# The first ninth of w1 in eight transfers of every eighth partition, instead of one transfer of 128 partitions

## The chip, the cores and the metric

One core of one Trainium2 chip runs the kernel. The metric is the device time of one execution in microseconds (us). The kernel before takes 136.42 us (median of 6 runs, 136.31 to 136.55). A run has a state, fast or slow; a run that is over 1.5% above the fastest of its kernel counts as slow. A ratio here is the mean time of one kernel's fast runs over the mean time of the other's fast runs of the same rounds, so it is not quite the ratio of the medians that are quoted. The span of a profile (134.6 us before) leaves out some 1.8 us at the ends.

## The reference, cut to what matters

One token passes through an attention branch and a feed-forward branch, mixed by a gate. All inputs are bfloat16.

```
x: [1, 1, 576]
g = sigmoid(sum(x * gate_w))
q = x @ wq                         # wq [576, 4096]
a = softmax(q k / sqrt(128)) v @ wo  # 16 KV heads, the last 4096 keys of each; wo [4096, 576]
h = gelu(x @ w1 + b1)              # w1 [576, 4608], 5.3 MB
b = h @ w2 + b2                    # w2 [4608, 576]
return g * a + (1 - g) * b
```

In all 53.6 MB have to be read once: K and V 33.6 MB, the four weights 20 MB. There is nearly no reuse, and reading sets the time: the profile below shows the DMA engines full from 4 us on, at 411 to 431 GB/s in the stretches listed up to 12 us.

## The kernel before: the parts that matter here

Four tiny loads go out on the scalar queue, all large ones on the sync queue, in this order. The first 512 rows of w1 are laid out as partition p, part k (row 4p + k). Each part is one load of 128 partitions x 4608 elements, 9216 B in a row.

```python
nc.scalar.dma_start(out=x_row[:], ...)      # 1 x 576
nc.scalar.dma_start(out=gw_row[:], ...)     # 1 x 576
nc.scalar.dma_start(out=b2_row[:], ...)     # 1 x 576
nc.scalar.dma_start(out=b1_t[:], ...)       # 128 x 2 x 18, runs of 36 B
...
w1_m = w1_t[:, 0 : KM * F].rearrange("p (k n) -> p k n", k=KM)        # KM = 4, F = 4608
w1_src = B_w1[0:DM, :].rearrange("(p k) n -> p k n", k=KM)
for k in range(KM):
    nc.sync.dma_start(out=w1_m[:, k, :], in_=w1_src[:, k, :])          # 1.18 MB each
nc.sync.dma_start(out=w1_l, ...)            # the last 64 rows of w1, 0.59 MB
... # wq: two loads of 2.1 MB, one of 0.5 MB; then 8 K loads, 8 V loads of 2.1 MB, w2 and wo
for r in range(0, RO, 8):                   # wo, late in the kernel: 4 loads of 1.18 MB, rows of 9216 B
    nc.sync.dma_start(out=wo_t[:, r : r + 8, :], in_=wo_src[:, r : r + 8, :])
```

The product h = x @ w1 uses part k for 36 matmuls, and each of them needs all 128 partitions of the part. So splitting a part by partitions does not let any product start earlier.

The framework that schedules the kernel gives each transfer on the sync and scalar queues one of eight completion semaphores, in turn. A transfer whose semaphore is still held by an earlier one waits in its issuing queue until that one has landed: in the kernel before the first wq load waited 2.7 us for w1 part 0, and the first K load 5.1 us for b1; by the trace each of the two pairs is on one semaphore.

## Time and profile before

| what | before |
|---|---|
| time | 136.42 us |
| bytes read | 53.6 MB, 398 GB/s over the span |
| first w1 row starts to move | 1.74 us |
| w1 part 0 has landed | 5.95 us |
| last large landing on the chain, then the tail | 127.47 us, then about 5 us of row products |

The view by stretches of the kernel before comes first. Its columns are the stretch in us and its length, busy us (and instructions) of each engine, then the granted TensorE clock, the mean busy share of the 16 DMA engines and the GB/s they moved. A packet, the piece that one engine moves at a time, counts whole in the stretch in which it starts.

```profile
1.00:2.00 1.00, 0.00 (x0) 0.00 (x0) 0.03 (x1) 0.00 (x0) 0.97 (x4) 1.00 0.34 66
2.00:4.00 2.00, 0.47 (x5) 0.31 (x5) 0.66 (x3) 1.71 (x2) 1.39 (x5) 1.00 0.91 309
4.00:6.00 2.00, 0.00 (x1) 0.01 (x1) 0.17 (x1) 1.53 (x1) 0.00 (x0) 1.00 0.99 416
6.00:8.00 2.00, 2.00 (x32) 2.00 (x33) 2.00 (x12) 0.00 (x0) 0.00 (x0) 1.00 1.01 416
8.00:10.00 2.00, 1.58 (x19) 1.48 (x17) 0.11 (x2) 0.00 (x0) 0.00 (x0) 1.00 1.05 431
10.00:12.00 2.00, 2.00 (x28) 1.79 (x29) 0.98 (x4) 0.17 (x1) 0.00 (x0) 1.00 0.99 411
...
100.00:120.00 20.00, 10.09 (x219) 7.80 (x217) 0.48 (x2) 0.00 (x0) 0.00 (x0) 0.50 1.00 420
```

From 4 us on the last two columns hardly move: the DMA engines are full, at 411 to 431 GB/s in these stretches. TensorE is idle for half of the stretch from 100 to 120 us. The kernel is bound by its loads, and no gap comes later in which a late start could be made up.

The timeline of the sync queue shows how little issuing it took to get there. Columns: start, busy us, queue, line, transfer, count.

```profile
0.74 2.03 SPq L77 DMA_DIRECT2D w_t<-in_B_w_dram  x4
2.82 0.47 SPq L78 DMA_DIRECT2D w_t<-in_B_w_dram  x1
5.97 0.82 SPq L85 DMA_DIRECT2D wq_t<-in_A_wq_dram  x2
6.83 0.46 SPq L86 DMA_DIRECT2D wq_t<-in_A_wq_dram  x1
```

By 3.3 us all 5.3 MB of w1, 12.5 us of transfer at 425 GB/s, are in the queue. Two lines, from the view of line 77 and from the waits of the sync queue, matter later:

```profile
L77 SPq DMA_DIRECT2D w_t<-in_B_w_dram x4: 384/426/649, 0.7 to 2.1; - x4
...
SPq L276 <- DMA b_t<-in_B_b_dram: 5.1, 1, 5.1
```

The first gives the duration of an issue (least, median, most, in ns). The second says that the first K load waited 5.1 us for the landing of b1 (256 packets of 36 B), whose semaphore it takes over. This wait cost nothing, as some 5.8 MB were still queued ahead when it ended. The chain of waits ends like this (start, us, what):

```profile
100.23 27.19 DMA w_t<-in_B_w_dram
127.47 0.28 PE ya_ps L184
```

### The profile page before, as it was taken

Reading aid. Unit: us, or ns where it says so; the run is one execution under the profiler, and the core shown is the slowest. Engines: PE = TensorE matmul, PEld = TensorE weight load, DVE = VectorE, ACT = ScalarE, POOL = GpSimd, SP = SyncE. Lnnn points to the kernel's source line nnn. Section 1 sums busy time; section 2 is a strip of 40 time slices with the busy share of each in tenths; the row PEclk is TensorE's granted clock in tenths of the full one; section 3 lists DMA queues with packets and bytes.
Section 4 is the critical chain, followed back from the end, with each engine's and each line's share of the span. In section 5 each row is a group of like instructions: output and inputs, shape, how many; then the busy total and the mean of one; then the engine's idle time right before and its main releaser. Section 6 shows DMA issues by size and latency. Waiting matters only on the chain.

```text
span 134.6 us, 2438 instructions
## 1 busy us (share of the span) xinstructions
PE 92.4 (69%) x1116; PEld 57.9 (43%) x1116; DVE 50.3 (37%) x65; ACT 6.8 (5%) x11; POOL 2.8 (2%) x13
## 2 busy tenths in 40 slices
PE   1289989570499798979679219799752253798692
PEld 0285983470133233323233018765652253455461
DVE  2242013012958999998984845200000000100001
ACT  3600000001000000000000060000000000000001
POOL 8000000000000000000000000000000000000000
PEclk9999999999999999999999975557975555569999
DMA  4999999999999999999999999999999999999940
GB/s 121 417 424 428 421 443 414 427 420 429 429 429 424 424 433 419 433 414 443 414 443 407 438 425 446 400 438 409 438 414 429 424 411 424 416 416 427 401 170 0
DMA packets 5041, 53.76 MB, mean 400 GB/s; under 512 B 804, under 2 KB 808, under 8 KB 1448
## 3 DMA queue, kind: packets, MB, share of 16 engines
q1 hardware_dynamic: 4754, 53.61, 94.8%
q8 instruction: 8, 0.13, 0.4%
q10 hardware_dynamic: 278, 0.01, 0.1%
q14 instruction: 1, 0.01, 0.0%
HBM read 53.62 MB, written 0.00 MB: 398 GB/s over the span
## 4 chain that ended last, share of the span: by engine, by line
DMA 69%; PE 14%; DVE 6%; issue 5%; SPq 3%; ACTq 1%; ACT 0%; DVEq 0%
DMA w_t<-in_B_w_dram 36%; DMA kv_t<-in_A_k_cache_dram 26%; DMA b_t<-in_B_b_dram 8%; DVE early L297 6%; PE s_ps L303 5%; PE ya_ps L184 4%; PE yb_ps L185 4%; SPq L400 2%; PE o_ps L384 1%; SPq L276 1%; ACTq L63 0%; ACT out_row L422 0%; ACTq L67 0%; ACTq L65 0%; DVEq L297 0%
## 5 line engine op out<-in xcount | busy, mean ns | idle before, releaser
L303 PE MATMUL s_ps<-early 128*128 128x512 bf16 x128 | 32.9, 404 | 11.3 <-DVE early L297 11.3
L297 DVE STREAM_TRANSPOSE early<-kv_t 128x2048 f32<-128x2048 f32 x16 | 35.8, 2286 | 5.4 <-DMA kv_t<-in_A_k_cache_dram 3.4
L303 PEld LDWEIGHTS <-early 128*128 128x128 bf16 x128 | 12.9, 100 | 30.9 <-issue 17.4
L384 PE MATMUL o_ps<-pt,kv_t 128*128 128x4 bf16 x512 | 15.0, 166 | 14.5 <-DMA kv_t<-in_A_v_cache_dram 10.8
L384 PEld LDWEIGHTS <-kv_t 128*128 128x128 bf16 x512 | 14.7, 103 | 15.2 <-DMA kv_t<-in_A_v_cache_dram 11.1
L194 PE MATMUL h_ps<-xt,w_t 128*128 128x1 bf16 x144 | 9.6, 201 | 3.6 <-DMA w_t<-in_B_w_dram 3.6
L406 DVE TENSOR_TENSOR om<-o_ps,rh 128x128 bf16<-128x128 f32 x1 | 0.3, 292 | 30.1 <-PE o_ps L384 30.1
L184 PE MATMUL ya_ps<-w_t,gt 128*1 128x288 bf16 x36 | 10.6, 324 | 1.4 <-DMA w_t<-in_B_w_dram 1.4
L194 PEld LDWEIGHTS <-w_t 128*128 128x128 bf16 x144 | 9.3, 162 | 4.7 <-DMA w_t<-in_B_w_dram 3.7
L185 PE MATMUL yb_ps<-w_t,gt 128*1 128x288 bf16 x36 | 10.5, 322 | 0.0
L184 PE MATMUL ya_ps<-wo_t,ov 128*1 128x288 bf16 x32 | 9.6, 328 | 0.7 <-DMA wo_t<-in_A_wo_dram 0.7
L185 PE MATMUL yb_ps<-wo_t,ov 128*1 128x288 bf16 x32 | 9.5, 326 | 0.0
L421 DVE CAST out_row<-ya_ps 1x288 bf16<-1x288 f32 x1 | 0.4, 446 | 16.1 <-PE ya_ps L184 16.1
L235 PE MATMUL q_ps<-xt,wq_t 128*128 128x1 bf16 x128 | 3.7, 165 | 1.8 <-DMA wq_t<-in_A_wq_dram 1.8
L185 PEld LDWEIGHTS <-gt 128*1 128x1 bf16 x36 | 3.4, 94 | 3.5 <-issue 1.6
L235 PEld LDWEIGHTS <-wq_t 128*128 128x128 bf16 x128 | 3.6, 104 | 2.7 <-DMA wq_t<-in_A_wq_dram 1.9
L337 ACT ACTIVATE early<-s_ps,negm 128x1024 bf16<-128x1024 f32 x2 | 2.2, 1108 | 47.2 <-DVE negm L332 47.2
L184 PEld LDWEIGHTS <-gt 128*1 128x1 bf16 x36 | 3.4, 94 | 2.0
L185 PEld LDWEIGHTS <-ov 128*1 128x1 bf16 x32 | 3.0, 95 | 2.4 <-issue 0.6
L184 PEld LDWEIGHTS <-ov 128*1 128x1 bf16 x32 | 3.0, 95 | 2.2 <-DVE ov L414 0.4
L285 PE MATMUL s_ps<-no_r,no_l 1*128 1x512 bf16 x8 | 3.6, 620 | 0.4 <-DVE hx L213 0.4
L213 DVE TENSOR_TENSOR hx<-h_ps,b_t 128x36 f32<-128x36 f32 x1 | 0.2, 196 | 8.1 <-PE h_ps L203 8.1
(78 smaller groups left out, 36.2 us busy)
## 6 DMA issues: line engine op xcount, KB each, us to landing
kv_t<-in_A_k_cache_dram SPq DMA_DIRECT2D x8, 2048.0 KB, 25.1
kv_t<-in_A_v_cache_dram SPq DMA_DIRECT2D x8, 2048.0 KB, 14.9
w_t<-in_B_w_dram SPq DMA_DIRECT2D x4, 1152.0 KB, 10.1
wo_t<-in_A_wo_dram SPq DMA_DIRECT2D x4, 1152.0 KB, 21.8
wq_t<-in_A_wq_dram SPq DMA_DIRECT2D x2, 2048.0 KB, 16.1
w_t<-in_B_w_dram SPq DMA_DIRECT2D x1, 2592.0 KB, 20.7
w_t<-in_B_w_dram SPq DMA_DIRECT2D x1, 1296.0 KB, 27.2
w_t<-in_B_w_dram SPq DMA_DIRECT2D x2, 576.0 KB
```

The source lines that it names most:

```text
L184: nc.tensor.matmul(ya_ps[:], lhsT=vec, rhs=row[:, 0:NH], start=start, stop=stop, skip_group_check=True)
L185: nc.tensor.matmul(yb_ps[:], lhsT=vec, rhs=row[:, NH:D], start=start, stop=stop, skip_group_check=True)
L194: nc.tensor.matmul(h_ps[:, c : c + 1], lhsT=w1_m[:, k, f0 : (c // NJ + 1) * FB : NJ], rhs=xt[:, k : k + 1], start=(k == 0 and c == 0), sto ...
L235: nc.tensor.matmul(q_ps[:, j : j + 1], lhsT=wq_m[:, k, j * Dh : (j + 1) * Dh], rhs=xt[:, k : k + 1], start=(k == 0 and j == 0), stop=False ...
L276: nc.sync.dma_start(out=t[:], in_=cache[0, 2 * i : 2 * i + 2, Sk - W : Sk, :].rearrange("h (p c) d -> p h (c d)", p=64),)
L285: nc.tensor.matmul(s_ps[:, n // 2, n % 2], lhsT=no_l[0:1, e, :], rhs=no_r[0:1, e, :], start=(e == 0), stop=False, skip_group_check=True,)
L297: nc.vector.transpose(out=kt.bitcast(FP32), in_=k_t[:, c1 * W : (c1 + 1) * W].bitcast(FP32))
L303: nc.tensor.matmul(s_ps[:, c1, n], lhsT=qz[:, i, j, :], rhs=kv[:, n, :, j // 2, :, j % 2], start=False, stop=(i == NPAIR - 1 and j == 3), ...
L337: nc.scalar.activation(out=p_x[:, c1 * 1024 : (c1 + 1) * 1024], in_=s_ps[:, c1].rearrange("p n k -> p (n k)"), func=ACT.Exp, bias=negm[:, ...
L384: nc.tensor.matmul(o_ps[:, 4 * i : 4 * i + 4], lhsT=v_t[:, c, :], rhs=pt[:, c, 4 * i : 4 * i + 4], start=(c == 0), stop=(c == 2 * NCH - 1),)
L400: nc.sync.dma_start(out=wo_t[:, r : r + 8, :], in_=wo_src[:, r : r + 8, :])
L421: nc.vector.tensor_copy(out=out_row[:, 0:NH], in_=ya_ps[:])
```

## The change

The intent, as the form of the change suggests: the first load of the kernel is cut so that each piece gives exactly one row to each of the 16 DMA engines, so that all of them start at once and short pieces land early.

```diff
-    for k in range(KM):
+    for p in range(8):
+        nc.sync.dma_start(out=w1_m[p::8, 0, :], in_=w1_src[p::8, 0, :])
+    for k in range(1, KM):
         nc.sync.dma_start(out=w1_m[:, k, :], in_=w1_src[:, k, :])
```

Bytes and 9216 B rows are the same. There are seven more transfers, of 147,456 B each.

## The prediction

> **What bounds the kernel now.** The DMA engines. The stretch-by-stretch view gives 416 to 428 GB/s from 4 us to 120 us; only the start (0 to 2 us: 33, 2 to 4 us: 309) and the last 4 us are not full. The chain of waits gives DMA 69%; its last piece is a w2 landing at 127.47 us, then 5 us of row products. So time lost at the head of the queue should reach the end one for one; no later gap absorbs it.
>
> **What the change does.** The first 1.18 MB of w1 was one issue (0.38 to 0.65 us on the sync queue), first data at about 2.1 us, landed 5.97 us. Now it is eight issues of 147 KB. Bytes, packets (9216 B, median 0.35 us each) and compute stay. Three effects:
>
> 1. Issue: at about 0.4 us each, eight issues take 3.2 us against 2.8 us of data at 425 GB/s.
>
> 2. Completion semaphores. The built program has eight, taken in turn by sync and scalar transfers. Before, the five w1 transfers issue almost without a wait. After, the 5th to 8th small ones wait for x_row, the first small one, gate_w and b2, and the second w1 part (k=1) waits for b1. b1 is 256 packets of 36 B. Before it landed at 12.36 us[...], and the first K load waited 5.1 us for it harmlessly behind a full queue. Now it gates the queue while only eight rows per engine are in front. It can finish only about when those rows run out, so the queue runs dry for 1.1 to 1.3 us from issue to first data (out row: issue 132.5, packet 133.6). I estimate a hole of 1 to 1.5 us.
>
> [...]
>
> **Sum.** [...]hole +1.3 us, b1 out of the way and smaller starts -0.4 us: about +3.4 us. [...] All on the critical path. I predict 139.4 us, range 137.1 to 140.6; faster by over 2%: 0.02, within 2%: 0.40, slower by over 2%: 0.58.
>
> **What would show it.** w1's first product starts near 8 us, not 6.0[...]. [...] The sync queue's waits name b1's landing before the k=1 issue, at about 8.4 us[...]; then the DMA share dips for about 1 us. The first K issue comes well before 12.38 us; from 12 us on everything runs later by a constant.
>
> **What would make it wrong.** [...] If b1's packets slip through small gaps between rows, b1 lands early and the hole vanishes. If the cold first packets (up to 1.15 us) get shorter, the head gains some tenths. A shift of TensorE's throttled stretches (0.5 from 100 to 120 us) into the last 5 us would add up to 2 us.

The sum came to about +3.4 us with a third term: +2.5 us, for the eight pieces moving at half rate. Without it the two terms that are left, +1.3 and -0.4 us, make +0.9 us; the author put that case at +1.1 us. The term was given a chance of 0.7, and the forecast was 139.4 us, 3.0 us over 136.42 us. The times near 8 us and about 8.4 us include it too. That b1 can finish only when the rows in front of it run out was the estimate; in the kernel before its 256 packets ran from 5.70 to 11.56 us, among rows of 0.347 us.

## The result, and the profile after

The changed kernel takes 139.69 us (median of 6 runs, 138.92 to 140.94) against 136.42 us. The ratio is 1.0246, with a 95% interval of 1.0201 to 1.0291. It is slower by 2.5%, and its times scatter more.

The same stretches of the changed kernel:

```profile
1.00:2.00 1.00, 0.00 (x0) 0.00 (x0) 0.02 (x1) 0.00 (x0) 0.97 (x4) 1.00 0.01 1
2.00:4.00 2.00, 0.47 (x5) 0.31 (x5) 1.19 (x4) 1.60 (x2) 1.39 (x5) 1.00 0.88 227
4.00:6.00 2.00, 0.14 (x1) 0.17 (x1) 1.72 (x12) 1.64 (x1) 0.00 (x0) 1.00 0.88 226
6.00:8.00 2.00, 0.62 (x3) 0.41 (x4) 0.98 (x4) 0.17 (x1) 0.00 (x0) 1.00 0.98 217
8.00:10.00 2.00, 2.00 (x7) 0.45 (x6) 0.00 (x0) 0.00 (x0) 0.00 (x0) 1.00 0.96 387
10.00:12.00 2.00, 2.00 (x36) 2.00 (x35) 0.00 (x0) 0.00 (x0) 0.00 (x0) 1.00 0.98 401
...
100.00:120.00 20.00, 10.06 (x301) 8.81 (x298) 0.48 (x2) 0.00 (x0) 0.00 (x0) 0.61 1.00 420
```

From 2 to 8 us the loads move at 217 to 227 GB/s, about half of before. From 12 us on the loads run at the same rate (425 and 424 GB/s from 12 to 20 us). Summed over the stretches from 1 to 12 us the kernel before moved 66 x 1 us + (309 + 416 + 416 + 431 + 411) x 2 us = 4.03 MB, the changed one 1 x 1 us + (227 + 226 + 217 + 387 + 401) x 2 us = 2.92 MB. The missing 1.11 MB are 2.6 us at 425 GB/s.

The sync queue's timeline, and the views of the lines that issue:

```profile
0.74 5.07 SPq L77 DMA_DIRECT2D w_t<-in_B_w_dram  x8
5.86 1.53 SPq L79 DMA_DIRECT2D w_t<-in_B_w_dram  x3
7.43 0.65 SPq L80 DMA_DIRECT2D w_t<-in_B_w_dram  x1
...
L77 SPq DMA_DIRECT2D w_t<-in_B_w_dram x8: 564/588/634, 0.7 to 5.2; - x8
```

The eight issues run back to back, 0.588 us each, one every 0.63 us (0.74, 1.41, 2.02, 2.70, 3.33, 3.96, 4.59, 5.23 us in the chain of waits). The second part of w1 is issued at 5.86 us. Before, it was issued at 1.18 us. There is no wait for b1 among the sync queue's waits in these 8 us: b1 had landed by 4.87 us. Its small packets now took 0.5 us in all (3.38 to 3.90 us), against 5.9 us before; presumably they find gaps between the rows.

The chain of waits now starts with those issues and ends as before, 3.05 us later at the last large landing (130.52 us against 127.47 us):

```profile
5.23 0.59 SPq L77
5.86 0.59 SPq L79
...
104.40 26.13 DMA w_t<-in_B_w_dram
130.52 0.04 issue
130.57 0.28 PE ya_ps L186
```

The trace also holds every DMA packet. The next table is worked out from those records, on the profile's own clock, as in the views. (A completion signal mostly follows its packet by 0.435 to 0.455 us, in this run as in the others, so packet times of different runs can be set side by side.) "Wave" means every 16th row of the first 128, in order of start; the share is the sum of packet times within the stretch over 16 engines (a little over 1 where packets of one engine overlap).

| w1 part 0 | before | after |
|---|---|---|
| first row starts | 1.74 us | 2.13 us |
| eighth wave starts | 4.89 us | 6.61 us |
| time from wave to wave | 0.45 us | 0.64 us |
| landed (last completion signal) | 5.95 us | 8.61 us |
| mean time of a row | 0.417 us | 0.559 us |
| DMA share from 2.5 to 5 us / 5 to 7.5 us | 1.01 / 1.02 | 0.88 / 0.92 |
| last w2 transfer ends on an engine, mean of 16 | 129.71 us | 132.27 us |
| the same, slowest engine | 130.19 us | 133.28 us |

The first ninth has landed 2.66 us later: 0.39 us because the first row starts later, 1.33 us between the waves, 0.94 us in the last wave and its landing. At the end of the kernel the mean engine is 2.56 us late and the slowest one 3.09 us. The span grew from 134.57 to 137.74 us, by 3.2 us, so it follows the slowest engine. In the changed kernel every wave starts 1.38 to 1.54 us after the start of its own issue (the first at 2.13 and 0.74 us, the eighth at 6.61 and 5.23 us): the waves keep step with the issues.

Two causes can make the head run at half rate, and this trace alone does not say what each is worth. Theory I is the issue pace: 147,456 B every 0.63 us is 234 GB/s. Theory P is the set of partitions: a piece that writes only some partitions, here every eighth, moves at a lower rate, whatever the pace of its issues. That is the assumption; with half rate assumed it gives some 212 GB/s (half of 425). Both are near the 217 to 227 GB/s that were seen.

### The profile page after: what moved, and what is told of

The parts are those of the page before. It is cut to its first block, busy times and chain, and to the rows that moved or that the text cites. A ratio compares the mean times of both kernels' runs of the same rounds, so it can differ in the third digit from the quotient of the medians.

```text
span 137.7 us, 2448 instructions
## 1 busy us (share of the span) xinstructions
PE 92.6 (67%) x1116; PEld 57.9 (42%) x1116; DVE 50.4 (37%) x65; ACT 6.9 (5%) x11; POOL 2.8 (2%) x13
## 4 chain that ended last, share of the span: by engine, by line
DMA 49%; PE 20%; DVE 12%; SPq 8%; issue 7%; ACT 1%; DVEq 0%
DMA kv_t<-in_A_k_cache_dram 30%; DMA w_t<-in_B_w_dram 19%; DVE early L299 8%; PE s_ps L305 6%; PE o_ps L386 5%; PE ya_ps L186 4%; PE yb_ps L187 4%; SPq L77 3%; SPq L402 2%; DVE pt L347 2%; DVE m_668 L317 2%; SPq L79 1%; ACT early L339 1%; SPq L87 1%; PE t_ps L359 1%
## 5 line engine op out<-in xcount | busy, mean ns | idle before, releaser
L305 PE MATMUL s_ps<-early 128*128 128x512 bf16 x128 | 32.4, 398 | 11.7 <-DVE early L299 11.6
L186 PE MATMUL ya_ps<-w_t,gt 128*1 128x288 bf16 x36 | 11.1, 335 | 1.0 <-DMA w_t<-in_B_w_dram 1.0
L187 PE MATMUL yb_ps<-w_t,gt 128*1 128x288 bf16 x36 | 11.1, 334 | 0.0
```

Of the source, the lines that this page charges most:

```text
L186: nc.tensor.matmul(ya_ps[:], lhsT=vec, rhs=row[:, 0:NH], start=start, stop=stop, skip_group_check=True)
L187: nc.tensor.matmul(yb_ps[:], lhsT=vec, rhs=row[:, NH:D], start=start, stop=stop, skip_group_check=True)
L305: nc.tensor.matmul(s_ps[:, c1, n], lhsT=qz[:, i, j, :], rhs=kv[:, n, :, j // 2, :, j % 2], start=False, stop=(i == NPAIR - 1 and j == 3), ...
```

## The experiments

Twelve kernels ran, each with three rounds beside the kernel before. The diffs are against the changed kernel unless it says otherwise. All gave correct results. Theory P's figures for pieces of every eighth partition assume half rate: 0.65 to 0.7 us is twice the 0.347 us that a 9216 B row takes in the kernel before, and 5.5 us is twice the 2.8 us of part 0.

### The same eight, in an order that alternates p and p + 4

```diff
-    for p in range(8):
+    for p in (0, 4, 1, 5, 2, 6, 3, 7):
```

> The eight small transfers are the same, only issued in the order 0,4,1,5,2,6,3,7[...]. Theory I (the issue of 0.59 us plus a gap, one every 0.63 us, sets the pace of the head; 147 KB in 0.63 us is 234 GB/s): the time stays at 139.7 us within 0.7, the second w1 part is still issued at 5.9 us; the row packets may get shorter. Theory P ([...]the issue takes 0.59 us only because the queue behind it is slow): rows fall from 0.56 toward 0.35 to 0.45 us, the issues quicken, and the time falls to about 137.5 us.

It took 139.07 us (138.90 to 139.28), ratio 1.0186 (1.0169 to 1.0203). The rows did get shorter, 0.493 us against 0.559 us, and the DMA share from 2.5 to 5 us and 5 to 7.5 us fell to 0.82 and 0.83. The issues stayed where they were, and so did the waves (6.63 us for the eighth). The stretch view shows that the shorter rows were turned into idle engines, not into bytes:

```profile
4.00:6.00 2.00, 0.26 (x2) 0.29 (x2) 1.60 (x12) 1.65 (x1) 0.00 (x0) 1.00 0.80 235
6.00:8.00 2.00, 0.62 (x3) 0.29 (x3) 0.98 (x4) 0.17 (x1) 0.00 (x0) 1.00 0.96 221
...
0.74 5.08 SPq L77 DMA_DIRECT2D w_t<-in_B_w_dram  x8
```

So the order of the pieces changes how long a row takes, 0.559 or 0.493 us, but the pace between waves is that of the issues. The 0.6 us that came back are at the end: the mean engine finished at 132.19 us, hardly earlier than in the changed kernel, the slowest at 132.77 instead of 133.28 us. (Each piece still writes the same 16 partitions; only their order is another.)

### Two issuing queues, pairs (p, p + 4) and pairs (p, p + 1)

```diff
-    for p in range(8):
-        nc.sync.dma_start(out=w1_m[p::8, 0, :], in_=w1_src[p::8, 0, :])
+    for p in range(4):                       # apart; shared: pairs (p, p + 1), p in 0, 2, 4, 6
+        nc.sync.dma_start(out=w1_m[p::8, 0, :], in_=w1_src[p::8, 0, :])
+        nc.scalar.dma_start(out=w1_m[p + 4 :: 8, 0, :], in_=w1_src[p + 4 :: 8, 0, :])
```

"Apart" stands for the pairs (p, p + 4), "shared" for the pairs (p, p + 1).

> Four of the small transfers (0 to 3) go out on the sync queue, four (4 to 7[...]) on the scalar queue, in pairs. Theory I: the issue pace doubles, head rows flow, second w1 part issued near 3.5 us; time 136.5 to 137.3 us. Theory P says the same[...]. If the two queues' issues slow each other down[...], it stays near 139.5 us.

> As the run with two queues apart, but even ones on sync and odd ones on scalar[...]. Theory I alone: same as the other two-queue run, 136.5 to 137.3 us, rows 0.35 to 0.45 us. [...]rows near 0.65 to 0.7 us, the first ninth takes about 5.5 us, time 138.5 to 139.2 us, 1.5 to 2 us over the run with two queues apart.

The last figures of the second text are those of theory P. Apart: 140.27 us (139.89 to 140.75), ratio 1.0264. Shared: fast runs of 140.34, 140.57 and 141.41 us, ratio 1.031. A fourth run of the shared one took 387.59 us; it counts as slow, its profile fell into it and is not used, and nothing here explains it. Both expectations of a gain failed, and so did the expected 1.5 to 2 us between the two.

In the trace of the one with pairs apart, sync issued its four by 3.84 us and scalar its four from 2.41 to 4.97 us, so the last issue ended 0.85 us earlier than in the changed kernel. The eighth wave started only 0.33 us earlier, at 6.28 us. Data came later after its issue than in the changed kernel: sync's fourth piece was issued at 3.35 us and started at 5.19 us, the second part of w1 was issued at 4.90 us and started at 7.07 us. That is 1.84 and 2.17 us, against 1.38 to 1.54 us, and it fits the third branch of the first expectation, that the two queues slow each other down (139.5 us; measured 140.27 us). Rows took 0.551 us. Later it lost more (341 and 332 GB/s from 8 to 10 and 10 to 12 us, against 387 and 401). The record shows two waits of the sync queue before that, 1.0 us for b1 and 0.7 us for a small piece of the scalar queue, and by the packets the engines stood idle for some 0.5 us between 6.5 and 8.5 us. Whether that is all, no run tests. A second queue is no remedy here (140.27 us against 139.69 us with one).

### Sixteen neighbouring partitions in each piece

```diff
-        nc.sync.dma_start(out=w1_m[p::8, 0, :], in_=w1_src[p::8, 0, :])
+        nc.sync.dma_start(out=w1_m[16 * p : 16 * p + 16, 0, :], in_=w1_src[16 * p : 16 * p + 16, 0, :])
```

> Eight transfers again, each of 16 neighbouring partitions[...]. Theory I: as the changed kernel, 139.7 us, rows at most 0.6 us. Theory P: [...]time 144 to 146 us. The issue duration tells whether it is the stride of 8 that makes it 0.59 us (then 0.4 here) or the 16 rows.

It took 142.49 us (141.66 to 142.95), ratio 1.0427. The issue view and the waits of the sync queue:

```profile
L77 SPq DMA_DIRECT2D w_t<-in_B_w_dram x8: 311/418/432, 0.7 to 4.9; - x8
...
SPq L79 <- DMA b_t<-in_B_b_dram: 2.6, 1, 2.6
...
6.00:8.00 2.00, 0.55 (x2) 0.50 (x2) 0.97 (x4) 0.17 (x1) 0.00 (x0) 1.00 0.82 106
8.00:10.00 2.00, 1.94 (x4) 0.33 (x4) 0.01 (x1) 0.00 (x0) 0.00 (x0) 1.00 1.08 138
```

Three things are told apart here. The issue takes 0.418 us, as for whole loads: it is the stride over partitions, not the number of rows, that makes it 0.588 us (two and four strided pieces of 64 and 32 rows, below, took 0.566 and 0.586 us). The first row also started early again (1.77 us; in the profiled kernels whose first transfer strides over partitions it started at 2.10 to 2.14 us, in the others at 1.74 to 1.79 us). And with quicker issues the head was slower: rows took about 1.1 us from the third wave on, and part 0 had landed only at 12.05 us. So the set of partitions matters, as theory P said: with the issues quicker, sixteen neighbours took about 1.1 us a row against 0.559 us for every eighth partition. How much was not foreseen: 144 to 146 us were expected. The wait for b1 that the prediction had feared appears here, 2.6 us. But it left no hole: by the packets the engines were busy throughout (a DMA share of 0.95 over the two stretches above), with rows that were still under way.

### Eight and four pieces by columns: each writes all 128 partitions

```diff
-    for p in range(8):
-        nc.sync.dma_start(out=w1_m[p::8, 0, :], in_=w1_src[p::8, 0, :])
+    for p in range(8):                       # the other kernel: 4
+        c = slice(p * F // 8, (p + 1) * F // 8)
+        nc.sync.dma_start(out=w1_m[:, 0, c], in_=w1_src[:, 0, c])
```

> Eight transfers of the same 147 KB, but each all 128 partitions by 576 columns (1152 B rows)[...]. Theory I: if the issue takes 0.59 us again, 139.2 to 139.9 us; if it is 0.4 us as for other 128-partition loads, 137.0 to 137.6 us. Theory P: 136.5 to 137 us whatever the issue. The 1152 B packets (0.048 to 0.054 us in the kernel before) are a little slower per byte, worth 0.3 to 0.5 us here.

> The first ninth in four column pieces (128 rows of 2304 B, 295 KB each)[...], against the four-transfer split by partitions (138.6 us). If a fixed cost per transfer at the head counts: eight column pieces cost 3.2 us, four should cost 1.0 to 1.8 us, 137.4 to 138.3 us. If the 1152 B rows alone made the loss of the eight pieces: 136.5 to 136.9 us, as 2304 B rows run at 0.094 us, 24.5 GB/s an engine.

Eight: 139.68 us (139.00 to 139.91), ratio 1.0222 (1.0193 to 1.0251). Four: 138.25 us (137.34 to 139.02), ratio 1.0104 (1.0037 to 1.0172). The eight missed both theories: with all 128 partitions in each piece and issues of 0.43 us it is as slow as the changed kernel. The stretch view of the eight:

```profile
2.00:4.00 2.00, 0.47 (x5) 0.31 (x5) 1.69 (x8) 1.71 (x2) 1.40 (x5) 1.00 0.95 236
4.00:6.00 2.00, 0.73 (x12) 0.76 (x13) 1.24 (x9) 1.53 (x1) 0.00 (x0) 1.00 0.92 242
...
0.74 3.72 SPq L78 DMA_DIRECT2D w_t<-in_B_w_dram  x8
```

The engines were nearly busy and yet moved 236 to 242 GB/s. Half of the 1152 B rows took 0.051 us, but the mean was 0.068 us: about one row in sixteen took over twice the median, up to 0.80 us. What holds these rows up, no run here shows. The pace of the issues, one every 0.47 us or 313 GB/s, explains only a part. Four pieces lose less than half of it. So small pieces at the head cost something by themselves, for a reason other than a stride over partitions or a part of the partitions.

### Two and four pieces by partitions

```diff
-    for p in range(8):
-        nc.sync.dma_start(out=w1_m[p::8, 0, :], in_=w1_src[p::8, 0, :])
+    for p in range(2):                       # the other kernel: 4, with p::4
+        nc.sync.dma_start(out=w1_m[p::2, 0, :], in_=w1_src[p::2, 0, :])
```

> Two transfers of every second partition (64 rows, four per engine[...]). Theory I: two issues of 0.4 to 0.6 us in place of one feed 590 KB each, no starving: 136.4 us within 0.4. [...]

> Four transfers of every fourth partition (32 rows, two per engine). Theory I: an issue every 0.63 us feeds 295 KB, 468 GB/s, just above what the engines take: 136.4 to 137.2 us. Theory P: [...]as in the changed kernel: 138.5 to 139.5 us.

Two: 136.68 us (136.56 to 136.84), ratio 1.0011 (0.9996 to 1.0027). Four: 138.59 us (137.25 to 139.03), ratio 1.0134 (1.0080 to 1.0187). An issue took 0.566 and 0.586 us. For two pieces theory I holds to 0.2 us: 590 KB behind each issue are enough, and 410 GB/s moved from 4 to 6 us. For four it expected at most 137.2 us, theory P at least 138.5 us. Its rows took 0.449 us, against 0.417 us in the kernel before; the mean engine finished 0.84 us late, the slowest 2.06 us late.

### The same split late in the kernel, behind a full queue

These three are the kernel before with the first wo load (same bytes, same rows as w1 part 0) split in eight, at a point where 14.8 to 18.9 us pass from the issue of a piece to its landing, so that the duration of an issue is hidden.

```diff
+        if r == 0:
+            for p in range(8):               # cols: wo_t[:, p : p + 1, :]; order: p in (0, 4, 1, 5, 2, 6, 3, 7)
+                nc.sync.dma_start(out=wo_t[p::8, 0:8, :], in_=wo_src[p::8, 0:8, :])
+            continue
         nc.sync.dma_start(out=wo_t[:, r : r + 8, :], in_=wo_src[:, r : r + 8, :])
```

> The kernel before, with the first of the four wo loads (same 1.18 MB, same 9216 B rows) split in eight of every eighth partition, late in the kernel, where over 10 us of transfers are queued ahead. Theory I: the issue cost is hidden, 136.4 us within 0.4, rows 0.35 us. Theory P: eight rows per engine at 0.69 instead of 0.35 us, that is +2 to +2.8 us, 138.4 to 139.2 us. Either way the issue's own duration (0.4 or 0.6 us) with the queue full tells whether it belongs to the form of the transfer or to the start of the kernel.

The first figures of the next two texts are for theory P.

> Control for the late split of wo, which lost 4.6 us: again eight transfers of 147 KB for the first wo load, with the same semaphore waits, but each of all 128 partitions by 576 columns (1152 B rows)[...]. [...]136.4 to 137.2 us (1152 B packets cost up to 0.5 us), no stretch under 330 GB/s near 112 to 120 us. If the eighth transfer's wait for the last V load made it: 139 to 141 us, with the same stretch of 150 to 250 GB/s.

> The late split of wo again, in the order 0,4,1,5,2,6,3,7. [...]part comes back, 138 to 140.3 us against 141.1; rows near 0.5 us in place of 0.6 to 1.05. If the number of transfers or their waits were the cause: 141.1 us within 0.5.

| first wo load | time, us | ratio | issue, median us | GB/s from 112 to 118 us |
|---|---|---|---|---|
| one transfer (the kernel before) | 136.47 and 136.79, by rounds | 1 | | 400, 419, 414 |
| eight, every eighth partition | 141.11 (140.60 to 141.40) | 1.0331 | 0.584 | 151, 175, 175 |
| the same, alternating order | 139.41 (139.08 to 140.40) | 1.0204 | 0.587 | 265, 231, 312 |
| eight, by columns | 137.79 (137.58 to 138.49) | 1.0090 | 0.427 | 321, 306, 406 |

The stretch from 114 to 116 us in these four kernels, in the order of the table:

```profile
114.00:116.00 2.00, 1.29 (x40) 1.14 (x38) 0.48 (x2) 0.00 (x0) 0.00 (x0) 0.50 1.01 419
```

```profile
114.00:116.00 2.00, 0.00 (x0) 0.00 (x0) 0.00 (x0) 0.00 (x0) 0.00 (x0) 0.50 0.84 175
```

```profile
114.00:116.00 2.00, 1.69 (x63) 1.70 (x64) 0.00 (x0) 0.00 (x0) 0.00 (x0) 0.50 0.74 231
```

```profile
114.00:116.00 2.00, 1.46 (x48) 1.26 (x45) 0.41 (x2) 0.00 (x0) 0.00 (x0) 0.50 1.00 306
```

All three split kernels have eight transfers with the same semaphore waits. Theory I alone said 136.4 us for the first and is out as the only cause. The loss goes with the partitions that are written, and with their order: 4.6 us for every eighth partition, 2.6 us for the same in alternating order, 1.0 us for pieces of all 128 (each against the median of its own rounds, 136.47, 136.79 and 136.79 us). In the first, packets of the V load that was still running were stretched too (the six that started from 112 to 114 us, from 0.61 us to 1.75 us on average); so a transfer of this form slows others beside it. It lost 4.6 us where doubling its own rows would have explained 2.8 us. Not all of the loss is slow rows: the eighth piece waits for the last V load (until 116.14 us in the first), and behind it the engines stood idle, by the packets 0.7, 0.5 and 0.25 us more in the three than in the kernel before (104 to 124 us). What is left still falls in the same order. The issue is as slow in the middle of the kernel as at its start.

### All of w1_m in eight pieces of every eighth partition

```diff
     for p in range(8):
-        nc.sync.dma_start(out=w1_m[p::8, 0, :], in_=w1_src[p::8, 0, :])
-    for k in range(1, KM):
-        nc.sync.dma_start(out=w1_m[:, k, :], in_=w1_src[:, k, :])
+        nc.sync.dma_start(out=w1_m[p::8, :, :], in_=w1_src[p::8, :, :])
```

The last figures are those of theory P.

> The same eight partition sets, but each transfer takes all four parts of w1_m (590 KB, four 9216 B rows or one longer run per engine), so an issue of 0.6 us feeds 1.4 us of data and the issue pace cannot bind. Issue pace as the cause of the changed kernel's loss: 136.4 to 137 us. [...]all 4.7 MB at about half rate, 7 to 11 us more, 143 to 147 us.

Its two fast runs took 148.39 and 150.10 us (two more, 150.67 and 151.35 us, count as slow by the rule); ratio of the fast ones 1.0911 (1.0812 to 1.1009). Each engine now moved one packet of 36,864 B per transfer, and those took 2.86 us. At the 0.347 us in which 9216 B move in the kernel before it would be 1.39 us. So in transfers of every eighth partition the same bytes take about twice as long, where the issues cannot be what limits (0.588 us each for 1.39 us of data). The sync queue waited 15.6 us for b1, whose packets lay between the slow rows (7.21 to 22.49 us) and which landed at 23.77 us:

```profile
SPq L78 <- DMA b_t<-in_B_b_dram: 15.6, 1, 15.6
...
14.00:16.00 2.00, 0.00 (x0) 0.00 (x0) 0.00 (x0) 0.00 (x0) 0.00 (x0) 1.00 0.35 74
```

The second line looks as if the queue had run dry, but it has not: few of these long packets start in that stretch. Taken by the time that packets were under way, the engines were 0.95 busy or more in every microsecond from 3 to 26 us, at some 205 GB/s. The next load's data started at 24.78 us, while the last rows of w1 were still moving, until 25.36 us. So the hole of the prediction did not open here either. The rate alone accounts for the loss: 4.72 MB take 11.8 us longer at 206 than at 425 GB/s, and the span of the profiled run grew by 11.7 us, a little over the 7 to 11 us that were expected from half rate.

What makes such a transfer slow is not shown. A piece that writes other partitions also reads other rows of w1, so no run parts the side that is written from the side that is read.

### What all runs have in common: the slowest engine

The lateness of the last w2 transfer on the 16 engines, against the kernel before, from the packet records of each profiled run, beside the growth of the span:

| kernel | mean engine, us | slowest engine, us | span, us |
|---|---|---|---|
| two by partitions | +0.4 | +0.5 | +0.5 |
| four by columns | +0.7 | +1.3 | +1.3 |
| eight by columns, late in wo | +0.7 | +1.1 | +1.2 |
| four by partitions | +0.8 | +2.1 | +2.1 |
| alternating order, late in wo | +2.0 | +2.7 | +2.9 |
| eight by columns | +2.2 | +3.2 | +3.4 |
| alternating order | +2.5 | +2.6 | +2.6 |
| the changed kernel | +2.6 | +3.1 | +3.2 |
| two queues, pairs apart | +3.4 | +4.2 | +4.4 |
| eight, late in wo | +4.6 | +4.7 | +4.8 |
| sixteen neighbours | +5.9 | +5.9 | +6.0 |
| all of w1_m | +11.7 | +11.7 | +11.7 |

The span follows the slowest engine to about 0.2 us everywhere, and the mean engine only where all are late alike. Why an engine that falls behind at the head stays behind to the end, no run tests. The changed kernel's times also scatter more: 2.0 us between the fastest and the slowest run of the changed kernel, 0.24 us before.

No version beat the kernel before.

## Why the prediction was right, point by point

The time was right: 139.4 us predicted, 139.69 us measured, slower as forecast. The critical path was right too: what the head lost came out at the end one for one, 2.6 us of missing bytes by 12 us and 2.56 us on the mean engine. The rest of the 3.2 us comes from engines drifting apart, which the prediction did not have. That the number is met to 0.3 us is luck. And the hole, +1.3 us of the sum, did not open, and the dearer issues, the later first row (0.39 us) and the slowest engine (0.5 us more than the mean), which the sum lacked, took its place.

- "At about 0.4 us each, eight issues take 3.2 us against 2.8 us of data." This step was mis-sized. The strided form takes 0.588 us, one every 0.63 us, so 8 x 0.63 = 5.0 us, and its first row starts 0.39 us later. This, not a small extra, sets the pace of the waves: 0.64 us from wave to wave. The evidence is that each wave starts 1.38 to 1.54 us after its own issue, and the run with the alternating order: shorter rows, more idle engines, the same pace. The duration 0.4 us had been taken from whole loads, and no strided load was in the trace.
- The term +2.5 us for half rate. That pieces of every eighth partition move at half rate is supported: 2.86 us against 1.39 us where the issue pace cannot bind, and the series late in wo. The mechanism is not shown. In the changed kernel itself the row took 0.559 us, 1.6 times 0.347 us and not twice. It is a second limit close to the first, and either alone would probably have cost a good part of the loss: the alternating order gave back 0.6 us, and the split with its issues hidden, late in wo, still lost 4.6 us. The two do not add: the issues alone allow 234 GB/s, pieces of every eighth partition alone moved 206 GB/s (16 packets of 36,864 B in 2.86 us), and together they left 217 to 227 GB/s.
- The hole behind b1, "+1.3 us". It did not happen in the changed kernel. The issue pace left gaps (DMA share 0.88 from 2.5 to 5 us), b1's packets slipped through them and landed by 4.87 us, which the prediction had named as its own way to fail. Where rows leave no gaps the wait for b1 is real, 2.6 us and 15.6 us in two of the runs, but the slow rows under way covered it and the engines did not run dry. The run with two queues did have idle engines after such a wait (1.0 us), but a second wait and late data came with it.
- "w1's first product starts near 8 us": it started at 9.80 us, but part 0 had landed at 8.61 us. The rebuilt program puts the gate and b2 products first on TensorE (7.80 to 9.87 us). This is off the critical path.
- What stays open: why pieces of every eighth partition, or of sixteen neighbours, are slow; why eight column pieces, without a stride and over all partitions, lose just as much; what makes single engines fall behind; how much of the two-queue versions' loss after 6 us their waits explain; and whether it is reading other rows or writing other partitions that slows the pieces.

## What to carry to other kernels

Where a kernel is bound by a full DMA queue, look at the shape of the very first transfers: what the head lost counted one for one here (2.6 us of bytes, 2.56 us on the mean engine). At the head 590 KB behind each issue cost nothing here, 295 KB cost 1.0 to 1.3%, 147 KB cost 1.9 to 4.3%. Late in the kernel pieces that span all 128 partitions lost least (0.9% against 3.3%), but at the head eight of them cost 2.2%. One row per engine does not mean full rate: pieces of every eighth partition moved 206 GB/s and pieces of sixteen neighbours 106 to 138 GB/s (from 4 to 10 us), where whole loads moved 411 to 431 GB/s. So measure the set of partitions before cutting a transfer by partitions. And before crediting or fearing a cost that is read from one form of a transfer, measure the form that will be used: a stride over partitions made the issue 40% longer here (0.588 against 0.418 us).
